# Gated linear attention and a channel mix: the first two 128-token groups joined into one of 256

## The chip, the cores and the metric

One core of one Trainium2 chip. The metric is device time of one execution in microseconds (us), median over runs; lower is better.

## The reference, cut to what matters

```python
# attention: batch 4, heads 8, sequence 768, head size 48
for t in range(S):
    state = alpha[:, :, t, :, None] * state + einsum('bhd,bhe->bhde', k[:, :, t], v[:, :, t])
    y[:, :, t] = einsum('bhd,bhde->bhe', q[:, :, t], state)
# channel mix on x = y as (4, 768, 384), d_ff 1024
x_prev = x shifted by one token
xk = mu_k * x + (1 - mu_k) * x_prev
xr = mu_r * x + (1 - mu_r) * x_prev
k = maximum(xk @ w_k, 0)
out = sigmoid(xr @ w_r) * (k * k @ w_v)
```

## The kernel before

The sequence is cut into chunks of `C` = 128 tokens (24 in all) and the chunks into attention groups (`CUTS`, L29): 13 groups, the first two of one chunk and the others of two. A group's `al`, `k`, `q` and `v` are loaded together (`attention_inputs`, L313). DVE forms running products of alpha by scans along the tokens (`forth` L365, `back` L409), one scan for each of the pairs of heads held, and scales q and k by them (L393). Four pairs of heads go on 128 partitions; three of them fill all rows, and the fourth is stored with its elements spread over the free rows of the three. SP's DMAs gather it into its own place after scaling (`gather`, L431). Group 0 is `DIRECT` (L33): its fourth pair comes straight from DRAM by six more small DMAs (`extra`, L334), and it has four scans each way.

Each chunk then has, on TensorE (PE): transposes of k (`trans` L468, copied out by ACT at L649); an entry, that is the update of the state sums (`update` L485) and the scores (`scores` L497); and a visit, the chunk's outputs (`intra` L513, `inter` L535). DVE masks the scores (L582), advances the state (L613 to L618) and, after a visit, adds the crossed part (`crossed` L570) to what ACT copied out (`leave` L560). For the first four chunks (`JOINED`) entry and visit are separate jobs, and the entry of the next chunk waits for the mask, the copy and the add of this one; later they are one job. Then `spread` (L579) moves the fourth pair's outputs to their partitions by two DMAs.

The channel mix works on groups of its own (`MOES`, L34): group 0 joins the first two attention groups, group 1 is one of 256 tokens, groups 2 to 6 have 512. Of each: a mix (ACT scale L790, DVE blend L793, ACT rounding L796, DVE remainder L799) for xk and for xr; 8 up products of 9 matmuls (`up_ops` L810: high and low halves of fp32 operands) into one of three PSUM tiles `pm`, with relu and squares on ACT (L816 to L822) and a remainder on DVE (L825); 3 gate products of 9 (L835); 3 down products of 24 (L847); and a multiplication by the gate and the store (L970, L975). The down products of group 0 and those after are as wide as the group. In group 0 the mix and the up products are made per attention group, so 128 columns at a time:

```python
            for a in segs:                                    # L1007
                n = GROUPS[a][2] * C
                up_jobs(g, n0, n, w, mix_jobs(g, 0, n0, n, w, [a]))
```

The weights come as raw 64-bit words in ten pieces (4 for w_k, 2 for w_r, 4 for w_v) and are converted in four steps each (`weights`, L729: ACT L744, DVE L752, ACT L760, DVE L764) through two buffers.

The order on every engine is fixed when the kernel is built. `Plan` (L67) holds jobs with an engine, an estimated duration, needs and ring buffers; `order` (L154) simulates them 60 times with varied priorities and keeps the shortest. Engines then run their queues in order. Dummy products on a zero tile keep PE active: `WARM` = 22 at the start (L235), and in every planned gap of PE up to a planned time of `QUIET` = 45 (L1055):

```python
            if plan.start[j] < QUIET and at > 0.0:
                for i in range(int((plan.start[j] - at - 0.2) / 0.2)):
                    PE.matmul(pms[2][:R, :R], zero, zero, start=True, stop=True)
```

Of the kernel before, what the change touches and what calls it, by code (L numbers as in the profile page):

```python
# [25 lines left out]
B, H, S, D = 4, 8, 768, 48  # L26
DM, FF = 384, 1024
C = 128
CUTS = [[1, 1, 2, 2], [2, 2, 2], [2, 2, 2], [2, 2, 2]]  # L29
GROUPS = [(b, sum(cut[:i]), n) for b, cut in enumerate(CUTS) for i, n in enumerate(cut)]  # L30
NA = len(GROUPS)
PLACE = [(0, 0), (0, 1)] + [(i, 0) for i in range(1, NA - 1)]
DIRECT = (0,)  # L33
MOES = [[0, 1], [2], [3, 4], [5, 6], [7, 8], [9, 10], [11, 12]]  # L34
NG = len(MOES)
LMAX = 2 * C
WMAX = 2 * LMAX
NP = H // 2
# [4 lines left out]
NT = 3  # L43
# [5 lines left out]
DW = D // DQ  # L49
NX = HB - D  # L50
NW = 768
WARM = 22
ROUNDS = 60
RAWS = 2
JOINED = 4
QUIET = 45.0


def head(i, o):
# [120 lines left out]
def mm(n):  # L180
    return 0.013 + n / 2400.0 if n > 128 else 0.068
# [6 lines left out]
def act(n, extra=0.0):  # L188
    return 0.13 + n / 1200.0 + extra
# [7 lines left out]
def gated_attention_channel_mix(  # L197
# [17 lines left out]
    PE, ACT, DVE, POOL, SP = nc.tensor, nc.scalar, nc.vector, nc.gpsimd, nc.sync  # L215
# [21 lines left out]
    als, pps, ks, qs = (ring(x, 2, [128, NP * LMAX]) for x in ("al", "pp", "k", "q"))  # L237
    vs = ring("v", 2, [C, 2 * VW])
    for t in (als[0], ks[0], qs[0]):
        POOL.memset(t[:, NT * C : NP * C], 1.0)  # L240
    tiny = cp.tile([128, 1], F32, name="tiny")
    POOL.memset(tiny, FLOOR)
    mone = cp.tile([128, 1], F32, name="mone")
# [32 lines left out]
    tops = [early[:, :NW], *ring("tops", 1, [128, NW], U32)]  # L276
# [19 lines left out]
    plan = Plan()  # L296
    add = plan.add
# [12 lines left out]
    loads, prepped, gathered, half_k, half_q, rescale = {}, {}, {}, {}, {}, {}  # L310
# [150 lines left out]
    def final(a):  # L461
        return a + 1 == NA or GROUPS[a + 1][0] != GROUPS[a][0]

    def trans(i):
        a, c = CH[i]
        k = view(a, ks)
        for p in range(NT):
            PE.transpose(pt[:, p, :], k[:, p, c * C : (c + 1) * C], ident)  # L468
# [141 lines left out]
    def advance(i):  # L610
        a, c = CH[i]
        old, new, nxt = before[i, 0], before[i, 1], marks[i]
        DVE.tensor_tensor(by_pair(new), by_pair(old), grown[:R, 0], op=ALU.add)  # L613
        if nxt is None:
            return
        DVE.tensor_tensor(by_pair(nxt), by_pair(new), grown[:R, 1], op=ALU.add)
        if c == GROUPS[a][2] - 1:
            DVE.tensor_tensor(  # L618
                by_pair(nxt), by_pair(nxt), pes[a % 2][:R].unsqueeze(2).to_broadcast([R, NP, D]),
                op=ALU.mult,  # L620
            )
# [4 lines left out]
    def attention_products():  # L626
        last_mask = last_leave = last_cross = last_adv = last_visit = None
        done = {}
        tcopy = {}

        def slow(i):
            return 1.3 if i < JOINED else 1.0

        def joined_at(i):
            return i >= JOINED

        for i in range(-1, NCH):
            more = i + 1 < NCH
            need = [last_mask, last_adv, last_leave, last_cross, last_visit]
            opened = ()  # L640
            if more:
                a, c = CH[i + 1]
                tr = add(
                    "PE", 0.32 * slow(i), lambda i=i: trans(i + 1), need=[prepped[a]],
                    takes=[("pt", i + 1)], uses=[("k", a)], name=f"trans{i + 1}",
                )

                def keep(i=i):
                    ACT.copy(hts[(i + 1) % 2].rearrange("t (r i) -> t i r", i=NT), pt)  # L649

                tcopy[i + 1] = add(
                    "ACT", act(NT * 128, -0.02), keep, need=[tr], takes=[("ht", i + 1)],
                    uses=[("pt", i + 1)], name=f"ht{i + 1}",
                )
                ready = [tcopy[i + 1], *half_k[a], *half_q[a], *loads[a]["v"]]
                touched = [("ht", i + 1), ("k", a), ("q", a), ("v", a)]
                opened = (0,) if marks[i + 1] is None else (0, 1)
            if i >= 0:
                mine = [("am", i), ("q", CH[i][0]), ("v", CH[i][0]), *before[i]]
            joined = i >= JOINED and more  # L660

            def visit(i=i, out=i >= 0, more=more, opened=opened if joined else ()):
                if more and joined_at(i):
                    update(i + 1, opened)
                if out:
                    intra(i, opened)
                    inter(i, 0)
                    inter(i, 1)
                if more and joined_at(i):
                    scores(i + 1)  # L670

            def enter(i=i, opened=opened):
                update(i + 1, opened)
                scores(i + 1)

            vis = None
            if i >= 0:
                need += ready if joined else []
                vis = add(
                    "PE", (2.28 if joined else 1.5) * slow(i), visit, need=need,  # L680
                    uses=mine + (touched if joined else []), name=f"visit{i}",
                )
                last_visit = vis
                a, c = CH[i]
                last_leave = add(
                    "ACT", 0.5, lambda i=i: leave(i), need=[vis], takes=[("xt", slot_of[a])], name=f"leave{i}"
                )
                last_cross = add(
                    "DVE", 0.42, lambda i=i: crossed(i), need=[vis, last_leave], uses=[("xt", slot_of[a])],
                    name=f"cross{i}",  # L690
                )
                done.setdefault(a, []).append(last_cross)
            if more and not joined:
                a, c = CH[i + 1]
                vis = last_visit = add(
                    "PE", 1.0 * slow(i), enter, need=[*ready, last_mask, last_adv, last_leave, last_cross, last_visit],
                    uses=touched, name=f"enter{i + 1}",
                )
            if more:
                last_mask = add(  # L700
                    "DVE", 0.62, lambda i=i: masked(i + 1), need=[vis], takes=[("am", i + 1)],
                    name=f"mask{i + 1}",
                )
                a, c = CH[i + 1]
                ending = c == GROUPS[a][2] - 1
                last_adv = add(
                    "DVE", 0.62 + (0.25 if ending and not final(a) else 0.0), lambda i=i: advance(i + 1),
                    need=[vis, last_adv, *(rescale.get(a, ()) if ending else ())],
                    takes=[("st", x) for x in held[i + 1]],
                    uses=[before[i + 1][0], *([("pe", a)] if ending else [])], name=f"state{i + 1}",  # L710
                )
            if i >= 0:
                a, c = CH[i]
                if c == GROUPS[a][2] - 1:
                    mv = add(
                        "SP", 0.2, lambda a=a: spread(a), need=done[a], uses=[("xt", slot_of[a])], name=f"spread{a}"
                    )
                    src = [] if GROUPS[a][1] == 0 else [done[a - 1][-1], xready[a - 1][0]]
                    pre = add(
                        "POOL", 0.25, lambda a=a: prefix(a), need=src, takes=[("xt", slot_of[a])],  # L720
                        uses=[("xt", slot_of[a - 1])] if src else [], name=f"prefix{a}",
                    )
                    xready[a] = [mv, *done[a], pre]


    converted = {}
    turn_w = [0]

    def weights(key, f, src, at, hi, lo):  # L729
        n = hi.shape[1] * hi.shape[2]  # L730
# [15 lines left out]
                raw.bitcast(BF16)[:, 4::4], AF.Copy,  # L746
            )

        hb = add("ACT", act(n), head_bits, need=[ld], takes=[("tops", i)], uses=[("raw", i)], name=f"top {key}{f}")

        def join():
            DVE.scalar_tensor_tensor(  # L752
# [139 lines left out]
        return j  # L892

    def up_jobs(g, n0, n, w, xr_):
        slow = 1.6 if g == 0 else 1.0
        for f in range(NF):
            i, pk = acc(n)
            ri = rn[0]
# [5 lines left out]
            def ops(f=f, pk=pk, r=r, k2=k2, dst=dst, xh=xh, xl=xl):  # L904
# [4 lines left out]

            prod, relu = up_ops(f, pk, xh, xl, r, k2, None, None)[:2]  # L910
            jp = pe_job(
                9 * mm(n) * slow, prod, [*xr_, *converted["k", f // 2]], takes=[("pm", i)], uses=[("xk", g)],
                name=f"up{g}.{f}+{n0}",
            )
            jr = add("ACT", act(n, -0.02), relu, need=[jp], takes=[("r", ri)], uses=[("pm", i)], name=f"relu{g}.{f}")
# [131 lines left out]
    for j in late:  # L1047
        plan.need[j] += [k for i in range(turn_w[0]) for x in ("tops", "raw") for k in plan.users[x, i]]

    todo = plan.order(sizes, ROUNDS)  # L1050
    POOL.tensor_scalar(nu, mu, -1.0, 1.0, op0=ALU.mult, op1=ALU.add)
    at = 0.0
    for j in todo:
        if plan.eng[j] == "PE":
            if plan.start[j] < QUIET and at > 0.0:  # L1055
                for i in range(int((plan.start[j] - at - 0.2) / 0.2)):
                    PE.matmul(pms[2][:R, :R], zero, zero, start=True, stop=True)
            at = plan.start[j] + plan.dur[j]
        plan.fn[j]()
    order.close()  # L1060

# [177 lines left out]
```

## Time and profile before

| | us |
|---|---|
| median of 3 runs | 366.55 (364.83 to 367.21) |
| the profiled execution | 367.48 |
| its span, first to last instruction | 365.8 |
| PE busy | 347.4 |
| DVE busy | 225.3 |
| ACT busy | 203.1 |

The profile follows one execution. Times in rows count from the start of the span. A matmul row gives start, duration and the number merged into it; products are pipelined, so their price is the distance between starts and not the duration. fp32 products that are not marked fp32r are recorded twice. PEclk is the clock granted to PE as a share of 2.4 GHz; 0.50 is 1.2 GHz.

### The profile page before, as it was taken

To read this page: it belongs to the slowest core of one execution; us is meant where nothing else is said; L and a number is where in the kernel's file an instruction comes from. 1 tells how busy PE (TensorE), PEld (TensorE's weight loads), DVE (VectorE), ACT (ScalarE), POOL (GpSimd) and SP (SyncE) were. 2 spreads that over 40 slices of the span, in tenths; PEclk is the share of its full clock that TensorE was granted. 3 is DMA by queue.
4 is the path that set the end of the run, shared out by engine and by line. 5 is a ranking of instruction groups with operands and counts; after the bars stand their busy time and mean duration, and the time that the engine had idled before them with its cause. 6 is when DMAs were issued, how large, how long until landed. Compare 5 with 4: busy or idle time off the path is not lost. (4 is left out here: it accounts for less than half of the span.)

```text
span 365.8 us, 10482 instructions
## 1 busy us (share of the span) xinstructions
PE 347.4 (95%) x4469; PEld 301.1 (82%) x4469; DVE 225.3 (62%) x453; ACT 203.1 (56%) x405; POOL 24.6 (7%) x63
## 2 busy tenths in 40 slices
PE   7497999999999999999999999999999999999991
PEld 7387999999999888888888888888888888888780
DVE  5897566587898954659934679517479312743000
ACT  2756565455874993318981349951269731787100
POOL 6110021010000300100000010000000000000000
PEclk9798555599999999999999999999999999999997
DMA  5997705243644202543203443005421001100011
GB/s 182 319 316 227 232 2 185 55 143 82 175 112 125 77 6 62 161 161 90 78 3 104 135 142 110 18 2 126 144 68 39 2 3 42 40 29 0 4 59 35
DMA packets 18295, 35.62 MB, mean 97 GB/s; under 512 B 3776, under 2 KB 9408, under 8 KB 18240
## 3 DMA queue, kind: packets, MB, share of 16 engines
q1 hardware_dynamic: 18096, 34.86, 31.6%
q8 instruction: 37, 0.61, 0.7%
q14 instruction: 18, 0.15, 0.2%
q10 hardware_dynamic: 144, 0.00, 0.0%
HBM read 26.69 MB, written 4.72 MB: 86 GB/s over the span
## 5 line engine op out<-in xcount | busy, mean ns | idle before, releaser
L810 PE MATMUL pm<-xkh,wkh 128*128 128x512 f32 (+2 forms) x192 | 52.5, 388 | 1.6 <-ACT xkh L796 1.6
L810 PE MATMUL pm<-xkl,wkh 128*128 128x512 f32 (+2 forms) x192 | 51.5, 383 | 0.0
L810 PE MATMUL pm<-xkh,wkl 128*128 128x512 f32 (+2 forms) x192 | 51.5, 383 | 0.0
L810 PEld LDWEIGHTS pm<-xkh,wkh 128*128 128x128 f32 x192 | 37.6, 223 | 7.2 <-ACT xkh L796 2.0
L847 PE MATMUL pm<-kb,wvh 128*128 128x512 f32 x120 | 42.2, 404 | 0.0
L810 PEld LDWEIGHTS pm<-xkl,wkh 128*128 128x128 f32 x192 | 38.0, 224 | 4.9
L810 PEld LDWEIGHTS pm<-xkh,wkl 128*128 128x128 f32 x192 | 38.1, 224 | 4.9
L816 ACT ACTIVATE r<-pm 128x512 f32<-128x512 f32 (+2 forms) x64 | 31.1, 486 | 18.4 <-PE pm L810 18.1
L847 PE MATMUL pm<-kha,wvh 128*128 128x512 f32 (+1 forms) x108 | 38.1, 353 | 0.0
L847 PE MATMUL pm<-kla,wvh 128*128 128x512 f32 (+1 forms) x108 | 37.0, 342 | 0.0
L847 PE MATMUL pm<-kha,wvl 128*128 128x512 f32 (+1 forms) x108 | 36.8, 341 | 0.0
L790 ACT ACTIVATE x<-xt,mu 128x512 f32<-128x512 f32 (+2 forms) x48 | 26.3, 609 | 18.4 <-DMA xt<-xt 17.6
L582 DVE TENSOR_TENSOR am<-sp,mask 128x512 f32<-128x512 f32 x24 | 16.5, 688 | 31.6 <-PE sp L497 31.5
L822 ACT ACTIVATE k<-r 128x512 f32<-128x512 f32 (+2 forms) x64 | 32.6, 516 | 1.5 <-DVE kla L825 1.0
L649 ACT COPY ht<-pt 128x384 f32<-128x384 f32 x24 | 16.3, 678 | 30.3 <-PE pt L468 30.2
L793 DVE SCALAR_TENSOR_TENSOR x<-xt,nu,x 128x512 f32<-128x512 f32 (+2 forms) x48 | 27.3, 612 | 5.7 <-ACT x L790 4.9
L825 DVE TENSOR_TENSOR kb<-k,kb 128x512 fp32r<-128x512 f32 x20 | 13.8, 692 | 24.4 <-ACT k L822 14.9
L560 ACT COPY xt<-yu 112x512 f32<-112x512 f32 x24 | 14.0, 584 | 24.6 <-PE yu L535 20.5
L847 PEld LDWEIGHTS pm<-kb,wvh 128*128 128x128 f32 x120 | 22.6, 188 | 5.1
L970 DVE TENSOR_TENSOR sig<-pm,sig 128x512 f32<-128x512 f32 (+1 forms) x21 | 12.8, 611 | 22.3 <-PE pm L847 17.4
L409 DVE TENSOR_TENSOR_SCAN pp<-al,pp 128x255 f32<-128x255 f32 (+1 forms) x40 | 26.3, 690 | 0.3
L365 DVE TENSOR_TENSOR_SCAN pp<-al,tiny 128x256 f32<-128x256 f32 (+1 forms) x40 | 23.6, 630 | 3.3 <-DMA al<-al_p 1.7
(90 smaller groups left out, 630.4 us busy)
## 6 DMA issues: line engine op xcount, KB each, us to landing
v<-v_p SPq DMA_DIRECT2D x11, 400.0 KB, 5.1
al<-al_p SPq DMA_DIRECT2D x11, 384.0 KB, 3.2
q<-q_p SPq DMA_DIRECT2D x11, 384.0 KB, 3.8
k<-k_p SPq DMA_DIRECT2D x11, 384.0 KB, 3.7
out<-sig SPq DMA_DIRECT2D x15, 256.0 KB, 2.1
early<-wk_p SPq DMA_DIRECT2D x4, 768.0 KB, 4.5
early<-wv_p SPq DMA_DIRECT2D x4, 768.0 KB, 4.8
q<-q SPq DMA_DIRECT2D x22, 48.0 KB, 2.3
```

What stands on the lines that cost most here:

```text
L365: DVE.tensor_tensor_scan(view(a, pps)[:, p], view(a, als)[:, p], tiny.to_broadcast([128, n]), initial=START, op0=ALU.mult, op1=ALU.max,)
L409: DVE.tensor_tensor_scan(pp[:, p, 0 : n - 1][:, ::-1], x, x, initial=pp[:, p, n - 1 : n], op0=ALU.mult, op1=ALU.bypass,)
L560: ACT.copy(x[:R].rearrange("r i (s t) -> r i s t", s=2), yu[:R, :, : NP * HC].rearrange("r s (i t) -> r i s t", i=NP),)
L582: DVE.tensor_tensor(ams[i % 2], sp[:, :, : NP * HC].rearrange("c j (p t) -> c j p t", p=NP), mask.unsqueeze(1).unsqueeze(1).to_broadcast([ ...
L649: ACT.copy(hts[(i + 1) % 2].rearrange("t (r i) -> t i r", i=NT), pt)
L790: ACT.activation(x, now, AF.Copy, scale=mu[:, i, t : t + 1])
L793: DVE.scalar_tensor_tensor(x, prev, nu[:, i, t : t + 1], x, op0=ALU.mult, op1=ALU.add)
L810: PE.matmul(pk, w[:, t, cols], x[:, t], start=part == 0 and t == 0, stop=part == 2 and t == NT - 1,)
L816: ACT.activation(r, pk, AF.Relu)
L822: ACT.activation(k2, r, AF.Square)
L825: DVE.tensor_tensor(lo, k2, hi.bitcast(F32), op=ALU.subtract)
L847: PE.matmul(pv, w[f // 2][:, f % 2, cols], x, start=f == 0 and i == 0, stop=f == NF - 1 and i == 2,)
```

## The change

Attention groups 0 and 1, of 128 tokens each, become one of 256, so that all twelve groups have two chunks. No group is `DIRECT`: group 0 holds three pairs like the others, has its fourth gathered, and each group has its own place in the load buffers. The channel mix keeps its seven groups of 256, 256 and five times 512 tokens; the first is now one attention group, mixed and multiplied 256 columns wide. The up products of group 0 are 72 matmuls in place of 144. Dummies: 20 at the start, then as many as fit between a planned time of 8.6 and the first job of PE, and none in later gaps. Some planned durations change, and with them the order.

```diff
-CUTS = [[1, 1, 2, 2], [2, 2, 2], [2, 2, 2], [2, 2, 2]]
+CUTS = [[2, 2, 2]] * 4
-PLACE = [(0, 0), (0, 1)] + [(i, 0) for i in range(1, NA - 1)]
-DIRECT = (0,)
-MOES = [[0, 1], [2], [3, 4], [5, 6], [7, 8], [9, 10], [11, 12]]
+PLACE = [(i, 0) for i in range(NA)]
+DIRECT = ()
+MOES = [[0], [1], [2, 3], [4, 5], [6, 7], [8, 9], [10, 11]]
-WARM = 22
+WARM = 20
+WARMED = 8.6
-QUIET = 45.0
     for t in (als[0], ks[0], qs[0]):
-        POOL.memset(t[:, NT * C : NP * C], 1.0)
+        POOL.memset(t[:, NT * LMAX :], 1.0)
...
-                    "PE", 0.32 * slow(i), lambda i=i: trans(i + 1), need=[prepped[a]],
+                    "PE", 0.26 * slow(i), lambda i=i: trans(i + 1), need=[prepped[a]],
-                    "ACT", act(NT * 128, -0.02), keep, need=[tr], takes=[("ht", i + 1)],
+                    "ACT", 0.61, keep, need=[tr], takes=[("ht", i + 1)],
-                    "DVE", 0.62 + (0.25 if ending and not final(a) else 0.0), lambda i=i: advance(i + 1),
+                    "DVE", 0.75 + (0.3 if ending and not final(a) else 0.0), lambda i=i: advance(i + 1),
-        hb = add("ACT", act(n), head_bits, ...
+        hb = add("ACT", act(n, 0.2), head_bits, ...
-        slow = 1.6 if g == 0 else 1.0
-                9 * mm(n) * slow, prod, [*xr_, *converted["k", f // 2]], ...
+                9 * mm(n), prod, [*xr_, *converted["k", f // 2]], ...
+    filled = set(plan.first["pm", 2])
     todo = plan.order(sizes, ROUNDS)
-    at = 0.0
+    at = WARMED
+    cold = True
     for j in todo:
         if plan.eng[j] == "PE":
-            if plan.start[j] < QUIET and at > 0.0:
-                for i in range(int((plan.start[j] - at - 0.2) / 0.2)):
+            if cold and at == WARMED:
+                for i in range(int((plan.start[j] - at) / 0.19)):
                     PE.matmul(pms[2][:R, :R], zero, zero, start=True, stop=True)
             at = plan.start[j] + plan.dur[j]
+            cold = cold and j not in filled
```

First place, PE from its start to the transposes of the third chunk, before. `zero` marks dummies, `pt` transposes, `yu` and `sp` the tiles of states, outputs and scores:

```order
L235 MATMUL pm_70<-zero 112x112 x22
L468 MATMUL pt<-ident,k_103 128x128 x3
L1057 MATMUL pm_72<-zero 112x112 x2
...
L497 MATMUL sp<-q_105,k_103 64x64 x16
L1057 MATMUL pm_72<-zero 112x112 x9
L513 MATMUL yu<-am_178,v_107 64x64 x16
...
L468 MATMUL pt<-ident,k_103 128x128 x3
L1057 MATMUL pm_72<-zero 112x112 x12
```

The same place of the change:

```order
L235 MATMUL pm_70<-zero 112x112 x20
L1058 MATMUL pm_72<-zero 112x112 x13
L468 MATMUL pt<-ident,k_101 128x128 x6
...
L497 MATMUL sp<-q_103,k_101 64x64 x16
L513 MATMUL yu<-am_176,v_105 64x64 x16
...
L497 MATMUL sp<-q_103,k_101 64x64 x16
L468 MATMUL pt<-ident,k_102 128x128 x3
```

All dummies now stand ahead of the first transposes. The two chunks of group 0 are transposed together, and the scores are followed at once by the visit. The visits of chunks 0, 1 and 2 and the entry of chunk 2 all stand ahead of the first up product; before it was the visits of chunks 0 and 1.

Second place, DVE from the mask of chunk 0 (`am`, L582) to the add behind its visit (`xt`, L570), before:

```order
L582 TENSOR_TENSOR am_178<-sp,mask 128x512
L752 SCALAR_TENSOR_TENSOR early<-early 128x768
L409 SCALAR_TENSOR_TENSOR pp_101<-al_99,pp_101 128x127
L365 SCALAR_TENSOR_TENSOR pp_102<-al_100,tiny 128x256
L393 TENSOR_TENSOR k_103<-k_103,pp_101 128x384
L764 TENSOR_TENSOR wkl_158<-early,wkh_154 128x768
L570 TENSOR_TENSOR xt_180<-xt_180,sp 112x2x64 x2
```

And of the change:

```order
L582 TENSOR_TENSOR am_176<-sp,mask 128x512
L402 RECIPROCAL pp_100<-pp_100 128x3
L752 SCALAR_TENSOR_TENSOR early<-early 128x768
L409 SCALAR_TENSOR_TENSOR pp_100<-al_98,pp_100 128x255 x3
L764 TENSOR_TENSOR wkl_156<-early,wkh_152 128x768
L570 TENSOR_TENSOR xt_178<-xt_178,sp 112x2x64 x2
```

Three scans back of 256 tokens now stand between the two, where there were one of 128, a scan forward and a scaling of k. Both orders have a weight operation and a subtraction of the weights there.

## Rows read from the trace of the kernel before

**Rows 1.** The page's head: the span of the profiled execution.

```profile
span 365.8 us, 10482 instructions
```

**Rows 2.** Busy time by stage, the whole span in five stretches. Columns: from and to (us), length, busy us of PE, PEld (weight loads), DVE, ACT, POOL with the number of instructions, then the granted clock of PE, the DMA share and GB/s.

```profile
0.00:33.57 33.57, 23.13 (x378) 21.62 (x379) 25.15 (x51) 17.84 (x30) 9.16 (x36) 0.90 0.81 261
33.57:74.40 40.83, 40.83 (x355) 40.12 (x356) 26.26 (x66) 24.60 (x79) 3.67 (x3) 0.50 0.43 133
74.40:119.20 44.80, 44.58 (x904) 43.32 (x903) 39.50 (x88) 28.76 (x70) 2.89 (x7) 1.00 0.45 123
119.20:358.20 239.00, 238.86 (x2838) 196.09 (x2836) 133.75 (x252) 131.92 (x230) 8.92 (x17) 1.00 0.22 65
358.20:365.80 7.60, 0.00 (x0) 0.00 (x0) 0.66 (x1) 0.00 (x0) 0.00 (x0) 0.70 0.13 42
```

**Rows 3.** The same view for PE alone around the steps of its clock. Columns: from and to, length, PE busy us and instructions, granted clock, DMA share, GB/s.

```profile
15.00:19.00 4.00, 3.98 (x76) 0.50 0.99 344
20.00:26.00 6.00, 6.00 (x157) 1.00 0.96 296
...
34.00:72.00 38.00, 38.00 (x344) 0.50 0.42 131
...
74.00:75.00 1.00, 1.00 (x9) 0.74 0.11 43
```

**Rows 4.** PE in order of time: start and duration in us, line, tiles, shape, how many; in brackets the idle time ahead and what ended it. Up products (L810) of group 0, then its gate products (L835) at either clock.

```profile
33.57 0.91 PE L810 MATMUL pm<-xkh,wkh 128*128 128x128 f32 x3 [1.64 <-ACT xkh L796]
34.27 0.84 PE L810 MATMUL pm<-xkh,wkl 128*128 128x128 f32 x3
34.91 0.84 PE L810 MATMUL pm<-xkl,wkh 128*128 128x128 f32 x3
...
72.06 0.95 PE L835 MATMUL pm<-xrh,wrh 128*128 128x256 f32 x3
72.81 0.84 PE L835 MATMUL pm<-xrh,wrl 128*128 128x256 f32 x3
73.45 0.84 PE L835 MATMUL pm<-xrl,wrh 128*128 128x256 f32 x3
...
76.97 0.50 PE L835 MATMUL pm<-xrh,wrl 128*128 128x256 f32 x3
77.31 0.50 PE L835 MATMUL pm<-xrl,wrh 128*128 128x256 f32 x3
```

**Rows 5.** The same view, the first row of a visit (L513) or an entry (L485) and the row that follows it, at the low and at the high clock.

```profile
56.52 1.13 PE L513 MATMUL yu<-am,v 64*64 64x64 f32 x32
...
58.44 0.90 PE L810 MATMUL pm<-xkh,wkh 128*128 128x128 f32 x3
...
66.31 0.97 PE L485 MATMUL yu<-v,ht 64*64 64x48 f32 x30
...
68.16 0.90 PE L810 MATMUL pm<-xkh,wkh 128*128 128x128 f32 x3
...
75.44 0.69 PE L513 MATMUL yu<-am,v 64*64 64x64 f32 x32
...
76.52 0.61 PE L835 MATMUL pm<-xrh,wrh 128*128 128x256 f32 x3
...
82.94 0.79 PE L485 MATMUL yu<-v,ht 64*64 64x48 f32 x30
...
84.22 0.38 PE L847 MATMUL pm<-kha,wvh 128*128 128x256 f32 x1
```

**Rows 6.** In order of time: the masks of chunks 0 and 1 on DVE, and the starts of their visits on PE. Dummies stood between them on PE.

```profile
18.39 0.68 DVE L582 TENSOR_TENSOR am<-sp,mask 128x512 f32<-128x512 f32 x1
...
20.88 0.69 PE L513 MATMUL yu<-am,v 64*64 64x64 f32 x32
...
28.18 0.69 DVE L582 TENSOR_TENSOR am<-sp,mask 128x512 f32<-128x512 f32 x1 [0.55 <-PE sp L497]
...
29.81 0.69 PE L513 MATMUL yu<-am,v 64*64 64x64 f32 x32
```

**Rows 7.** In order of time: SP's issue of two of the six small loads of the fourth pair and of the load of k of group 0, and the scaling of that k on DVE.

```profile
1.72 1.33 SPq L334 DMA_DIRECT2D al<-al_p  x2
...
5.94 0.44 SPq L327 DMA_DIRECT2D k<-k_p  x1
...
13.79 0.69 DVE L393 TENSOR_TENSOR k<-k,pp 128x512 f32<-128x512 f32 x1
```

**Rows 8.** Groups of DVE's instructions by line and shape over the span: scans forward (L365) and back (L409), and remainders of the up products (L825). Columns: busy us in all and mean ns of one, then idle time ahead.

```profile
L409 DVE TENSOR_TENSOR_SCAN pp<-al,pp 128x255 f32<-128x255 f32 x33 | 23.3, 737 | 0.2
L365 DVE TENSOR_TENSOR_SCAN pp<-al,tiny 128x256 f32<-128x256 f32 x33 | 21.0, 675 | 1.2 <-DMA al<-al_p 1.2
...
L825 DVE TENSOR_TENSOR kla<-k,kha 128x128 fp32r<-128x128 f32 x16 | 4.3, 284 | 0.3 <-ACT k L822 0.3
...
L825 DVE TENSOR_TENSOR kla<-k,kha 128x256 fp32r<-128x256 f32 x8 | 3.2, 414 | 0.0
...
L365 DVE TENSOR_TENSOR_SCAN pp<-al,tiny 128x128 f32<-128x128 f32 x7 | 2.6, 414 | 2.1 <-POOL st L263 1.5 <-DMA al<-al_p 0.6
```

**Rows 9.** In order of time: SP's issue of the two moves of the fourth pair's outputs (L579) behind chunk 0, and the first reader that waited for them, on POOL (in brackets its idle time ahead).

```profile
23.50 1.28 SPq L579 DMA_DIRECT2D xt<-xt  x2
...
30.34 0.19 POOL L555 COPY xt<-xt 128x3 f32<-128x3 f32 x1 [3.94 <-DMA xt<-xt]
```

More of the change, by code (lines that the diff above doesn't have):

```diff
@@ L747, in head_bits @@
             )
-        hb = add("ACT", act(n), head_bits, need=[ld], takes=[("tops", i)], uses=[("raw", i)], name=f"top {key}{f}")
+        hb = add("ACT", act(n, 0.2), head_bits, need=[ld], takes=[("tops", i)], uses=[("raw", i)], name=f"top {key}{f}")
         def join():
@@ L911, in up_jobs @@
             jp = pe_job(
-                9 * mm(n) * slow, prod, [*xr_, *converted["k", f // 2]], takes=[("pm", i)], uses=[("xk", g)],
+                9 * mm(n), prod, [*xr_, *converted["k", f // 2]], takes=[("pm", i)], uses=[("xk", g)],
                 name=f"up{g}.{f}+{n0}",
```

## Prediction

> **What bounds the kernel now.** I read the stages of the span first [rows 1, 2]. TensorE (PE) is busy in every microsecond from 33.57 us, the first product of the channel mix, to 358.2 us; 7.6 us of close follow. So the end is set by when that dense stretch starts, by the work in it, and by the clock it runs at. The clock column is the second thing to see: from 33.57 to 74.40 us it reads 0.50, the 1.2 GHz level, and DVE is busy for only 26.26 of those 40.83 us. From 119.20 us on, where the products are 512 columns wide, everything runs at 1.00 with DVE at 56%, and the change does not touch that part. Whatever it does is done before 119.20 us.
>
> Then the clock in finer steps [rows 3]. It is 0.50 from 15 to 19 us, 1.00 from 20 us after dummy products, and 0.50 from 34 to 72 us, in which PE's busy share is 38.00 of 38. Being busy alone did not raise it. What runs there are the products of group 0, 128 columns wide. It rises between 74 and 75 us, 2 to 3 us after the first 256-wide products (the gate's, 72.06 us [rows 4]).
>
> Third, the price of one product [rows 4]. Three 128-wide products at the low clock start 0.64 us after the three before them (34.27 to 34.91): 0.213 us each. Three 256-wide ones at the low clock: also 0.64 us (72.81 to 73.45). Three 256-wide ones at 1.00: 0.34 us (76.97 to 77.31), 0.113 us each; I use 0.117, a little above. So a 128-wide product costs as much as a 256-wide one, and a change of width halves the bill.
>
> **The change part by part.** Group 0 now has 256 tokens in one piece. Its up products were 8 x 9 for each half, 144 at 0.213 us = 30.7 us. They become 72 at 0.117 us = 8.4 us: 22.3 us go. Both other products of the group (gate 27, down 72) keep count and width.
>
> In the dense stretch the low clock also slowed other work. An entry of a chunk (state update and scores) takes 66.31 to 68.16 = 1.85 us at the low clock, 82.94 to 84.22 = 1.28 us at the high one; a visit (the outputs) 56.52 to 58.44 = 1.92 us against 75.44 to 76.52 = 1.08 us [rows 5]. The entry of chunk 3 and 9 gate products (9 x 0.096) gain 0.6 + 0.9 = 1.5 us. Entry and visit of chunk 2 and the transposes of chunks 2 and 3 stood in the stretch (2.0 + 2.05 + 0.5 + 0.9 = 5.5 us, with gaps and three dummies); in the new order they stand ahead of the first up product. From the first up product to the last DVE operation it was 358.2 - 33.6 = 324.6 us; it becomes 324.6 - 22.3 - 1.5 - 5.5 = 295.3 us, if the clock is high and PE never waits.
>
> Low clock at the start of the stretch. Without dummies in the gaps I expect 1.2 GHz there. While it lasts, each microsecond does 0.117/0.213 = 0.55 us of work. It lasted 2.5 us with 256-wide products (72.06 to about 74.5, where the mean of 0.74 puts the step) and up to 5 us with dummies (15 to 20 us): 0.45 x 2.5 = 1.1 to 0.45 x 5 = 2.3 us. I take 1.6.
>
> Start of the stretch. Before, 33.57 us, and it needed only the first 128 tokens. Now it needs both chunks. Followed through the new order with durations from the rows: the small loads of the fourth pair are gone, so k is the fourth transfer on SP's queue instead of the tenth (issued at 5.94 us); its scaling on DVE (before 13.79 us) can end near 11 us, after three scans forward, the scaling of q, three scans back and one weight operation [rows 7, 8]. The fourth pair is now gathered by SP after that. This is an added wait: the third weight piece, k of group 1 and its v stand behind it on SP and are issued from some 12.4 us on, about when the third piece went before; and the last scores wait for the gather to land at 14 to 15 us. Entry 0 ends near 16 us, mask 0 near 17.7 us (DVE is full until then; before 19.07). Before, PE sat behind dummies: mask 0 ended at 18.39 + 0.68 = 19.07 and visit 0 began at 20.88 us, mask 1 at 28.87 and visit 1 at 29.81 us [rows 6]: 1.8 and 0.9 us that go. Against that, two entries and two visits run at the low clock, 2 x 0.57 + 2 x 0.84 = 2.8 us. These two nearly cancel. What does not cancel is DVE: between mask 0 and the add behind visit 0 there are now a weight operation, three scans back and a subtraction (0.9 + 3 x 0.7 + 0.9 us), so that add ends near 22 us, entry 1 near 24, visit 1 near 27.6, its add near 29 us. The move of the fourth pair to its partitions took from 23.50 to 30.34 us until its reader went on [rows 9]; with fewer loads ahead of it I take 3.5 to 4 us: it is there at 33 us. Scale, blend and round for three 256-wide tiles, two engines in turn, are some 4 us: first up product at 37 us. Ends: 33.6 (as before) and 41: DVE was busy for 25.15 of the first 33.57 us, 75%; the new order puts some 6 us more of DVE work ahead of this product (three forward scans, mask and state of chunk 2, the last weight halves, a mix twice as wide), and 31/0.75 = 41.
>
> New waits in the stretch. With PE faster, DVE is next. Until 119.20 us it was busy for 25.15 + 26.26 + 39.50 = 90.9 us. The change takes off four scans each way (seven 128-wide forward scans at 0.41 become three at 0.68, back alike), half the remainders (16 x 0.28 to 8 x 0.41) and some mixing: about 5 us [rows 8]. 86 us from 3 us on, at the 88% of the third stage (39.50/44.80), puts the first 512-wide product at 101 us, at 95% at 94 us. PE alone would be there at 37 + 60 = 97 us. I take 3 us of waiting for the pair of them (0 to 6), most likely ahead of the first down product, which needs the last converted weights.
>
> The six removed transfers are small but take SP 1.3 us of issue a pair, 4 us before 8 us [rows 7]; that is in the start above. POOL clears tiles twice as wide, ahead of the first load's landing: nothing, or 0.3 us. The planner's changed costs only reorder.
>
> Sum, in the profiled execution's time: 37 + 295.3 + 1.6 + 3 = 336.9 us to the last DVE operation, + 7.6 of close = 344.5 us span, + 1.7 (367.48 against a span of 365.8) = 346.2 us. That execution was 0.9 us above the median of the runs, so **345 us** against 366.55: 21.5 us or 5.9% less.
>
> The Trainium skill ("TensorE: Matmul & The Clock Gate", "What's actually happening") says that the gate follows how busy PE has been. The 38 us at 0.50 with PE full [rows 3] do not show that for busy time. The same page ("Seeing it yourself") reports the gate stuck at a low level for a long time; by that the low stage would be a stay of the gate that any product can meet, the second rival below.
>
> **Rivals.** (1) DVE sets the pace as poorly as it did: with its share up to 119.20 us, 90.9/119.2 = 76%, its 86 us end at 113 us, and the rest (239.0 us less one visit and entry, 2.3 us, that now come earlier) ends at 349.7: 358 us as a run. For it: waits of DVE for transfers and ACT stay. Against: half of its idle time was waiting for the slow PE. 15%.
> (2) The low clock lasts as long as before, 40.8 us from the first up product: 0.45 x 40.8 = 18.4 us in place of 1.6: 362 us. Against: 256-wide products ended it before within 2.5 us. 3%. **Slower**: the clock stays low until the 512-wide products; 58 us of work take 58/0.55 = 106 us, 48 us more: 391 us. It decides from 51 us of low clock on (0.45 x 51 = 21.5 + 1.6). 2%.
> (3) All is hidden: start at 33.6, no waits, 1 us of clock: 338 us. 15%.
>
> **How the numbers follow.** The forecast with its bounds (start 33.6 to 41, waits 0 to 6) has 65%, rivals 1 and 3 15% each, 2 5%. The range 338 to 355 us reaches from rival 3 to start 41 with waits 6 and a second fall of the clock (41 + 295.3 + 2 x 2.3 + 6, and 8.4 from there to the time of a run); most of rival 1 and all of 2 lie outside. A measurement tells about 1% (3.7 us) from no change; faster by more than that: 0.95, within: 0.03, slower: 0.02.
>
> **What would show it.** Right: up products of group 0 in 72 at some 0.117 us, clock 1.00 from 2 to 5 us after the first of them, that one at 36 to 38 us, the first 512-wide product at 97 to 101 us, DVE over 85% busy between them. Wrong: clock 0.50 beyond 45 us; the first up product after 41 us; PE idle for over 6 us between the two marks; or the stretch from 119.20 us grown from its 239 us less 2.3.

## The result, and the profile after the change

The changed kernel takes **348.08 us** (median of four runs, 346.2 to 348.18) against 366.88 us before (364.83 to 367.96, four runs on the same chip): a ratio of 0.9488 with a 95% interval of 0.944 to 0.9537, so 18.8 us or 5.1% less. 345 had been forecast, with a range of 338 to 355. The profiled execution took 346.2 us, as forecast for it; it was the fastest of its runs, so that the median lies 1.9 us above it and not 0.9 below.

On two chips of the experiments, 5 of 19 executions of the kernel before ended at 358.0 to 360.6 us at a mean clock of 0.947 to 0.954 in place of 0.93, by which they ran some 14 to 19 us less at 1.2 GHz (an estimate from clock and span; no trace of one was kept), so medians of all executions are used for that kernel below, not ratios, except where one is given, and against these shorter ones alone the run called kick gains 7.0 us in place of 12.0.

The page after, answering to [rows 1]: span, busy time by engine, and the granted clock in 40 slices of 8.6 us.

```profile
span 344.5 us, 10124 instructions
...
PE 320.7 (93%) x4345; PEld 273.4 (79%) x4345; DVE 221.1 (64%) x421; ACT 197.3 (57%) x367; POOL 20.4 (6%) x60
...
PEclk9755599999999999999999999999999999999997
```

The stages after, as in [rows 2]: the start to the first up product, the low clock, the rest of the up and gate products of group 0, the stage to the first 512-wide product, and from there to the last DVE operation. Columns: length; busy us of PE, weight loads, DVE, ACT, POOL, each with its instructions; clock; DMA share; GB/s.

```profile
0.00:39.91 39.91, 24.50 (x462) 21.55 (x463) 31.69 (x55) 22.20 (x36) 8.46 (x36) 0.66 0.81 274
39.91:43.56 3.65, 3.65 (x17) 3.65 (x18) 3.65 (x9) 3.65 (x6) 0.00 (x0) 0.50 0.64 217
43.56:56.12 12.56, 12.56 (x215) 12.16 (x215) 12.49 (x25) 12.34 (x32) 0.00 (x0) 1.00 0.75 226
56.12:101.78 45.66, 43.63 (x948) 42.10 (x947) 39.33 (x87) 28.67 (x70) 4.10 (x7) 1.00 0.42 116
101.78:338.34 236.56, 236.36 (x2709) 193.89 (x2707) 133.24 (x250) 130.48 (x227) 7.86 (x17) 1.00 0.22 65
```

In the dense stretch the 40.83 us at 0.50 of [rows 2] have become 3.65 us; ahead of it the mean clock is lower than before, 0.66 in place of 0.90, since no dummies stand in the gaps there (0.87 with them, in a run below). The dense stretch starts 6.3 us later than before, yet the first 512-wide product, the mark behind which nothing was to change, comes at 101.78 in place of 119.20 us: 17.4 us of the gain are there. The stage behind it is 236.56 us, the 239 before less one visit and entry, 2.4 us. Another 1.4 us are in the close after the last DVE operation, 6.2 us in place of 7.6. The span is 21.3 us shorter; the medians differ by 18.8, since the profiled execution before lay above its median and this one below.

The up products of group 0 after, answering to [rows 4]: start, time, engine, line, tiles, count.

```profile
39.91 1.01 PE L810 MATMUL pm<-xkh,wkh 128*128 128x256 f32 x3 [1.53 <-ACT xkh L796]
40.71 0.84 PE L810 MATMUL pm<-xkh,wkl 128*128 128x256 f32 x3
41.35 0.84 PE L810 MATMUL pm<-xkl,wkh 128*128 128x256 f32 x3
...
45.55 0.50 PE L810 MATMUL pm<-xkh,wkl 128*128 128x256 f32 x3
45.89 0.50 PE L810 MATMUL pm<-xkl,wkh 128*128 128x256 f32 x3
```

Start to start, three products take 0.64 us up to the rise of the clock and 0.34 after it: the two prices of the forecast, now for twice the tokens.

### The profile page after: what moved, and what is told of

The parts are those of the page before. It is cut to its first block, busy times and chain, and to the rows that moved or that the text cites. A ratio compares the mean times of both kernels' runs of the same rounds, so it can differ in the third digit from the quotient of the medians.

```text
span 344.5 us, 10124 instructions
## 1 busy us (share of the span) xinstructions
PE 320.7 (93%) x4345; PEld 273.4 (79%) x4345; DVE 221.1 (64%) x421; ACT 197.3 (57%) x367; POOL 20.4 (6%) x60
## 4 chain that ended last, share of the span: by engine, by line
PE 70%; DMA 9%; DVE 9%; ACT 7%; issue 2%; POOL 1%; SPq 1%; ACTq 0%; DVEq 0%
PE pm L847 24%; PE pm L810 24%; PE pm L835 9%; PE yu L485 3%; PE yu L513 3%; DMA xt<-xt 2%; PE sp L497 2%; DMA early<-wk_p 2%; DMA al<-al_p 2%; DMA mu<-mu_p 2%; PE pt L468 2%; ACT x L790 2%; DVE pp L409 2%; PE sp L535 1%; PE yu L535 1%
## 5 line engine op out<-in xcount | busy, mean ns | idle before, releaser
L810 PE MATMUL pm<-xkh,wkh 128*128 128x512 f32 (+1 forms) x168 | 43.8, 370 | 1.5 <-ACT xkh L796 1.5
L810 PE MATMUL pm<-xkh,wkl 128*128 128x512 f32 (+1 forms) x168 | 42.8, 364 | 0.0
L810 PE MATMUL pm<-xkl,wkh 128*128 128x512 f32 (+1 forms) x168 | 42.6, 362 | 0.0
L790 ACT ACTIVATE x<-xt,mu 128x512 f32<-128x512 f32 (+1 forms) x42 | 25.2, 654 | 28.0 <-DMA xt<-xt 28.0
L810 PEld LDWEIGHTS pm<-xkh,wkh 128*128 128x128 f32 x168 | 29.6, 193 | 6.8 <-ACT xkh L796 1.7
L810 PEld LDWEIGHTS pm<-xkh,wkl 128*128 128x128 f32 x168 | 29.9, 193 | 5.0
L816 ACT ACTIVATE r<-pm 128x512 f32<-128x512 f32 (+1 forms) x56 | 29.5, 530 | 7.6 <-PE pm L810 6.9
L810 PEld LDWEIGHTS pm<-xkl,wkh 128*128 128x128 f32 x168 | 29.8, 192 | 4.9
L822 ACT ACTIVATE k<-r 128x512 f32<-128x512 f32 (+1 forms) x56 | 31.5, 565 | 3.2 <-DVE kla L825 2.3
L825 DVE TENSOR_TENSOR kb<-k,kb 128x512 fp32r<-128x512 f32 x20 | 13.9, 693 | 24.2 <-ACT kb L819 12.9
L582 DVE TENSOR_TENSOR am<-sp,mask 128x512 f32<-128x512 f32 x24 | 16.4, 683 | 17.8 <-PE sp L497 17.8
L793 DVE SCALAR_TENSOR_TENSOR x<-xt,nu,x 128x512 f32<-128x512 f32 (+1 forms) x42 | 26.4, 665 | 1.5 <-ACT x L790 1.3
L847 PEld LDWEIGHTS pm<-kb,wvh 128*128 128x128 f32 x120 | 22.6, 188 | 5.0
L365 DVE TENSOR_TENSOR_SCAN pp<-al,tiny 128x256 f32<-128x256 f32 x36 | 22.8, 675 | 4.8 <-DMA al<-al_p 4.8
L409 DVE TENSOR_TENSOR_SCAN pp<-al,pp 128x255 f32<-128x255 f32 x36 | 25.2, 736 | 0.5 <-DVE pp L402 0.2
```

Source lines behind the costliest of these rows:

```text
L365: DVE.tensor_tensor_scan(view(a, pps)[:, p], view(a, als)[:, p], tiny.to_broadcast([128, n]), initial=START, op0=ALU.mult, op1=ALU.max,)
L409: DVE.tensor_tensor_scan(pp[:, p, 0 : n - 1][:, ::-1], x, x, initial=pp[:, p, n - 1 : n], op0=ALU.mult, op1=ALU.bypass,)
L582: DVE.tensor_tensor(ams[i % 2], sp[:, :, : NP * HC].rearrange("c j (p t) -> c j p t", p=NP), mask.unsqueeze(1).unsqueeze(1).to_broadcast([ ...
L790: ACT.activation(x, now, AF.Copy, scale=mu[:, i, t : t + 1])
L793: DVE.scalar_tensor_tensor(x, prev, nu[:, i, t : t + 1], x, op0=ALU.mult, op1=ALU.add)
L810: PE.matmul(pk, w[:, t, cols], x[:, t], start=part == 0 and t == 0, stop=part == 2 and t == NT - 1,)
```

## Experiments

Every kernel is an edit of the one before or of the changed one. The summary (medians; T is the start of the first up product, M that of the first 512-wide one, in each profiled execution). They were run on several chips; medians of the kernel before differ between chips by up to 2.3 us (364.55 to 366.88), and T differs by 0.2 us between the changed kernel's two traces:

| kernel | what differs | us | T | M |
|---|---|---|---|---|
| changed | | 348.1 | 39.91 | 101.78 |
| changed, again | other chip | 348.1 | 40.11 | 103.11 |
| halves in group 0 | changed, 128 wide there | 369.5 | 40.06 | 125.08 |
| halves in group 1 | changed, 128 wide there | 353.1 | 40.10 | 108.25 |
| kick | before, 20 dummies inside group 0 | 352.5 | 33.28 | 107.18 |
| dummies alone | before, the new rule | 367.0 | 33.77 | 118.69 |
| dummies in gaps | changed, the old rule | 348.5 | 40.88 | 103.74 |
| wide alone | before, up products 256 wide | 359.0 | 37.58 | 109.33 |
| all but the joining | before, wide, dummies, costs | 353.4 | 44.11 | 107.26 |
| old costs | changed, old planner costs | 352.0 | 40.70 | 103.80 |
| factors later | changed | 346.4 | 39.39 | 101.42 |
| join later | changed | 347.2 | 39.22 | 102.61 |
| spread first | changed | 348.8 | 40.00 | 106.30 |

**Width: halves in group 0.** The theory was that 128-wide products cost double per token and leave the clock low; the rival, that the joined groups and the start had made the gain.

```
-                    PE.matmul(pk, w[:, t, cols], x[:, t], ...)
+                    for z in halves:      # columns 0:128, 128:256, in group 0 only
+                        PE.matmul(pk[:, z], w[:, t, cols], x[:, t, z], ...)
```

> The changed kernel, but each up product of group 0 is made as two of 128 columns: 144 instead of 72, in the same jobs, with every other engine's instructions in the same order. My theory (a 128-wide product costs what a 256-wide one costs at the 1.2 GHz level, and as long as they run the clock stays there): the clock reads 0.50 from the first up product (39.9 us) until 2 to 4 us into the gate products, each product takes 0.213 us, 30.7 us in place of 8.4, and entry, visit and gate products beside them run at the low clock too (1.5 to 2.5 us): 348 + 24 = 372 us, between 367 and 376. Rival (the gain came from the joined attention groups and the start, the clock rises whatever runs): the clock rises within 5 us, and 144 products at 0.06 to 0.117 us cost 8.6 to 16.8 us: 348 to 357 us.

369.46 us (368.68 to 373.25): 21.4 us back, as my theory had it and not the rival; 22.3 were forecast for count and clock together, and some 1.5 for what runs beside these products. (Both halves are summed side by side in one bank, which changes the sums of that group; what is timed is the products.) Busy PE and clock:

```profile
50.00:60.00 10.00, 10.00 (x48) 0.50 0.41 120
60.00:70.00 10.00, 10.00 (x75) 0.50 0.14 39
70.00:78.00 8.00, 8.00 (x76) 0.50 0.44 115
78.00:80.00 2.00, 2.00 (x19) 0.98 0.00 0
```

The reader sees PE full and the clock at 1.2 GHz for 38 us, from T on, as in [rows 3], in a kernel that differs from the changed one in product width alone. The Trainium skill ("TensorE: Matmul & The Clock Gate", "What's actually happening") lets the clock follow how busy PE has been; here equal busy shares stand beside either level, so PE's busy time as the profile records it does not tell the level in these rows.

**Halves in group 1**, the same edit with `g == 1`, entered at the high clock.

> The changed kernel, but the up products of group 1 (not 0) are made in halves of 128 columns, entered with the clock at 1.00. My theory (these products do not hold the clock): it falls back to 0.50 within the 144 products, which then take 0.213 us each: 10 to 22 us more, 358 to 371 us. Rival (the clock has only to be raised once and stays): it reads 1.00 throughout, the products take 0.06 to 0.117 us: 0 to 8.4 us more, 348 to 357 us; the price of a 128-wide product at 2.4 GHz is then read from their starts.

353.14 us (352.4 to 353.8), 5.0 more: the rival was right, and my theory's second half fell. The clock did not fall back:

```profile
72.00:76.00 4.00, 4.00 (x38) 1.00 0.21 80
76.00:80.00 4.00, 4.00 (x144) 1.00 0.19 26
80.00:84.00 4.00, 4.00 (x38) 1.00 0.56 204
84.00:88.00 4.00, 4.00 (x38) 1.00 0.13 25
```

The 128-wide products in that stretch, six to a row:

```profile
72.48 0.83 PE L811 MATMUL pm<-xkh,wkh 128*128 128x128 f32 x6
73.15 0.83 PE L811 MATMUL pm<-xkh,wkl 128*128 128x128 f32 x6
73.82 0.83 PE L811 MATMUL pm<-xkl,wkh 128*128 128x128 f32 x6
```

0.67 us for six is 0.112 each, beside 0.113 to 0.117 for a 256-wide one. So at either level a 128-wide product costs what a 256-wide one costs, and in these two kernels such products neither raised nor lowered the clock. Of the 8.1 us that 72 products more cost at 0.112, 5.0 show in the time: PE waits less, 0.4 us from T to M in place of 2.0.

By these prices the change of group 0 is 144 x 0.213 - 72 x 0.112 = 22.6 us. How it splits depends on the order: with the clock first, 144 x (0.213 - 0.112) = 14.5 us are the clock's and 8.1 the count's; with the count first, 72 x 0.213 = 15.3 are the count's and 7.3 the clock's. Why a 128-wide product costs as much as one of twice the width stays open. The profile records a weight load beside each product ([rows 2]: 356 beside 355), and no run here tells the load from the product.

**Clock alone: the kick.** If that is so, a push inside the stretch (dummy products that raise the clock) must give most of the clock's 14.5 us with no change of width.

```
+        if plan.name[j] == "up0.2+0":          # kernel before
+            for i in range(20):
+                PE.matmul(pms[2][:R, :R], zero, zero, start=True, stop=True)
         plan.fn[j]()
```

> The kernel before, with 128-wide up products throughout; the only edit is 20 dummy products (112 columns) put ahead of the third up product group of group 0, inside the dense stretch. My theory after the two halves runs (128-wide products keep the clock at whichever level it is, and cost 0.213 or 0.112 us by it): the dummies take 2.5 to 4 us, the clock rises behind them some 7 us after the first up product and stays, 126 products save 0.101 us each (12.7 us) and the entries, visits and gate products beside them 2 to 3 us: 367 + 3.5 - 15 = 355 us, between 351 and 361, with no change of width at all. Rival (128-wide products pull the clock down again): 366 to 371 us.

352.52 us (351.2 to 355.19), against a median of 364.55 for the kernel before on that chip: 12.0 less. From T to M its trace has 73.90 us, where that of the kernel before has 85.63: 11.7 less. The products around the dummies:

```profile
36.06 0.84 PE L810 MATMUL pm<-xkl,wkh 128*128 128x128 f32 x3
36.70 6.01 PE L1061 MATMUL pm<-zero 112*112 112x112 f32 x40
42.48 0.53 PE L810 MATMUL pm<-xkh,wkh 128*128 128x128 f32 x3
42.85 0.50 PE L810 MATMUL pm<-xkh,wkl 128*128 128x128 f32 x3
43.18 0.49 PE L810 MATMUL pm<-xkl,wkh 128*128 128x128 f32 x3
```

And the clock:

```profile
33.28:40.00 6.72, 6.72 (x36) 0.54 0.67 192
40.00:42.00 2.00, 2.00 (x19) 0.84 0.88 273
42.00:44.00 2.00, 2.00 (x22) 1.00 1.03 418
44.00:61.50 17.50, 17.50 (x315) 1.00 0.37 115
```

The dummies cost 5.8 us, more than the 2.5 to 4 I gave them; the clock rises within them, the same 128-wide products then go at 0.33 in place of 0.64 us per three, and it stays up. One edit of three lines gives nearly two thirds of the change's gain.

So 128-wide products stay at the low clock once they have it; what brought it is another question. In the kernel before it was high up to the first of them (columns as in [rows 3]):

```profile
32.00:33.00 1.00, 0.00 (x0) 1.00 0.76 252
33.00:34.00 1.00, 0.43 (x2) 0.78 0.76 172
```

It fell within half a microsecond of T, behind a stop of PE of 1.64 us ([rows 4]); in the kick, too, it was high up to T and fell there. With dummies up to T in the changed kernel (the old rule, below) it did not fall. But the changed kernel also has a stop of 1.68 us ahead of 89.69 us, at 1.00, and no fall behind it. So what brings the fall is not shown, and the kernel before with its stop filled was not run.

**The dummies' rule.** In the kernel before the new rule alone (20, then up to the first transposes); in the changed one the old rule added (`plan.start[j] < 45.0`, up to the first product into the third `pm` tile).

> The kernel before with the change's rule for dummies alone: 20 and then as many as the plan leaves up to the first transposes, none in later gaps. My theory: group 0 stays at 0.50 for some 40 us as before; visits no longer stand behind dummies (1.8 and 0.9 us), entries and visits run at the low clock (2.8 us): 363 to 370 us, middle 367. Rival (the dummies in the gaps cost the time): under 362 us.

366.99 us; the ratio to the kernel before is 1.0026 (1.0002 to 1.0049): same, as costed. Here the clock was at 0.50 ahead of T already, and the low stage ended as before, near 74 us.

> The changed kernel with dummy products in the gaps of the early visits again, by the rule of the kernel before (68 of them after the first transposes). My theory: the clock is high in the entries and visits and at the first up product (1.6 us of low clock go, 2.8 us in visits and entries of which about half is on the path), but visits stand behind dummies for 1 to 2 us: 345 to 350 us, middle 347. Rival (the dummies are what held the kernel before): 351 us or more.

348.46 us (348.41 to 349.28), no change. Its dense stretch, and that of the changed kernel as run again:

```profile
40.88:103.74 62.86, 59.36 (x1176) 56.66 (x1177) 54.30 (x116) 43.63 (x104) 3.71 (x7) 1.00 0.50 141
```

```profile
40.11:103.11 63.00, 60.67 (x1177) 58.46 (x1178) 55.73 (x118) 44.73 (x106) 3.94 (x7) 0.96 0.48 142
```

With the clock high from the first product PE is busy 1.3 us less, and the stretch is as long: PE waits 3.5 us in place of 2.3. So what is left of the low clock is hidden behind waits for inputs, and DVE, busy for 54.30 of the 62.86 us, is not far behind PE.

**Width alone** in the kernel before: both mixes, then `up_jobs(g, 0, w, w, mixed)`.

> The kernel before with one edit alone: the up products of group 0 are made once, 256 wide, after both 128-token mixes; attention groups of one chunk, the fourth-pair loads and the dummies in gaps stay. My theory (width and clock carry the gain): 72 products at 0.117 us, clock high from 2 to 5 us after the first (or at once, behind dummies), first up product 37 to 41 us: 344 to 355 us, middle 349. Rival (joining the attention groups carries it): over 358 us.

358.97 us (358.19 to 361.49), in the rival's range (over 358) and 10 us above the middle of mine: 7.2 us below the kernel before on that chip (366.15). PE between T and M, its busy time and clock (columns as in the stages above):

```profile
37.58:109.33 71.75, 64.57 (x1182) 62.36 (x1183) 61.83 (x131) 48.68 (x114) 3.96 (x9) 0.91 0.48 141
```

And its costliest wait (us in all, times, longest):

```profile
PE yu L485 <- ACT ht L649: 7.1, 4, 4.2
```

PE waited 7.1 us for the transposed k of later chunks, and the clock was low for some 13 of the 71.75 us: 6.3 us from T on, and again from 54 to 61 us, behind the longest of these waits. T is 2.3 us earlier than in the changed kernel and M 7.6 later. So width alone does not carry the gain: it needs inputs that come in time.

**All but the joining**: that edit, the new dummies and the new planner costs.

> The kernel before with wide up products of group 0, and also the change's dummies and planner costs: all of the change but the joining of the first two attention groups and the fourth-pair loads. My theory after the run with wide products alone (359 us; PE waited 7 us for the inputs of later attention groups and the clock was low for some 6 us): the joined groups give the rest, 355 to 361 us. Rival (dummies and costs gave the rest): 347 to 351 us.

353.44 us (352.43 to 354.94): just under the range of my theory and above the rival's. Ahead of its first up product PE stood still:

```profile
40.48 0.90 PE L469 MATMUL pt<-ident,k 128*128 128x128 f32 x3 [9.47 <-DVE k L394]
43.56 0.90 PE L469 MATMUL pt<-ident,k 128*128 128x128 f32 x3 [2.18 <-ACT ht L650]
44.11 0.99 PE L811 MATMUL pm<-xkh,wkh 128*128 128x256 f32 x3
```

The transposes of chunk 2 wait in PE's queue, and the products behind them, for DVE to scale k of a third group; joined, chunk 2 is the second group's. From T to M it takes 63.15 us, like the changed kernel's 63.00, and M to the last DVE operation 236.9 against 236.5. So the joining, with the fourth pair's loads that go with it, is worth 4.0 us at T and 1.6 in the close (from the start of the last DVE operation to the end of the span: 351.7 - 344.1 = 7.6, against 345.6 - 339.6 = 6.0): 5.6, where the medians say 5.3.

**The planner's costs** of the kernel before in the changed one (0.32 for the transposes, 0.62 for the states, `act(n)` for the tops, 1.6 on the up products).

> The changed kernel with the planner's costs of the kernel before (transposes, hidden-state copy, states, tops, factor 1.6 on the up products of group 0), which gives another order on every engine. My working put these costs at nothing: 346 to 350 us. Rival (the costs carry part of the gain): 351 us or more.

351.95 us (350.78 to 352.06), so 3.8 us hang on them. The rival was right. Its two stages, T to M and from M on:

```profile
40.70:103.80 63.10, 58.53 (x1048) 56.26 (x1049) 55.71 (x119) 44.26 (x105) 4.22 (x7) 0.97 0.47 140
103.80:343.41 239.61, 238.95 (x2838) 196.00 (x2836) 133.35 (x250) 131.13 (x229) 7.58 (x17) 1.00 0.22 65
```

As many microseconds to M, but with 129 matmuls fewer: one visit and entry stay behind M, and the last stage is 3.1 us longer. The costs "only reorder", and the order is worth 1%.

**The start of the stretch: three trials.** First, POOL's mixing factors issued behind `ends1`, so that DVE's reciprocal needn't wait for POOL, which waits for their load.

> The changed kernel; POOL's product of the mixing factors (which waits 1.62 us for their load) is issued behind the ends of group 1 instead of ahead of the ends of group 0, so that DVE's reciprocal of group 0 need not wait for it. My theory (this wait of 1.37 us is what put the scaling of k 1.5 us behind the time I forecast, and the start of the stretch hangs on the chain behind it in part): the scaling of k ends at 11.1 instead of 12.5 us, and the first up product comes 0.3 to 1.4 us earlier: 346.7 to 347.8 us. Rival (the chain is held by the landing of the fourth weight piece and of the spread): no change of the start, 348 us.

346.42 us (346.01 to 347.01), the best kernel of the study. In the changed kernel:

```profile
7.68 0.20 POOL L1051 TENSOR_SCALAR nu<-mu 128x6 f32<-128x6 f32 x1 [1.62 <-DMA mu<-mu_p]
...
8.40 0.18 DVE L402 RECIPROCAL pp<-pp 128x3 f32<-128x3 f32 x1 [1.37 <-POOL pe L383]
...
32.42 1.29 SPq L579 DMA_DIRECT2D xt<-xt  x2
...
36.73 0.51 ACT L790 ACTIVATE x<-xt,mu 128x256 f32<-128x256 f32 x1 [2.70 <-DMA xt<-xt]
```

And with the factors later:

```profile
7.64 0.18 DVE L402 RECIPROCAL pp<-pp 128x3 f32<-128x3 f32 x1 [0.40 <-POOL pe L383]
...
31.10 1.29 SPq L579 DMA_DIRECT2D xt<-xt  x2
...
36.20 0.51 ACT L790 ACTIVATE x<-xt,mu 128x256 f32<-128x256 f32 x1 [3.12 <-DMA xt<-xt]
```

The spread [rows 9] goes out 1.3 us earlier and is used 0.5 earlier. (The median is 1.7 us below the changed kernel's, more than T moved, but from another chip: how much of that is the edit's isn't settled.) So the transfer holds a part back; does it wait for those queued ahead of it? The next run moves it ahead of them.

> The changed kernel; on SP the spread of group 0 to its partitions is issued ahead of the loads of q and v of group 2 instead of behind them, nothing else is moved. My theory (the start of the dense stretch at 39.9 us hangs on the landing of the spread, 4.3 us after its issue, because 784 KB stand ahead of it): the spread lands 1 to 2 us earlier, the first up product is at 38 to 39 us, 346 to 347.5 us against 348.1. Rival (the start hangs on mask 2 and visit 2, or on the mix itself): the first up product within 0.4 us of 39.9 and 348 us, or slower by the later q and v.

348.82 us (347.61 to 350.88), T 40.00: no gain in time. But the transfer did get shorter:

```profile
33.19 1.91 SPq L579 DMA_DIRECT2D xt<-xt  x2
...
36.82 0.51 ACT L790 ACTIVATE x<-xt,mu 128x256 f32<-128x256 f32 x1 [2.62 <-DMA xt<-xt]
```

From issue to use it took 3.6 us, where it takes 4.3 and 4.9 us in the two traces of the changed kernel. So the loads ahead of it cost some 0.7 to 1.3 us; T did not follow, because in this execution the spread went out 0.8 us later (33.19 for 32.42), as k of group 0 was already scaled 0.5 us later. PE's waits from T to M grew to 4.0 us, at transposed k and at the mix; whether the later q and v of group 2 did that is not shown. What makes up the 3.6 us that are left, for two moves of 48 KB, stays open.

> The changed kernel with POOL's mixing factors behind the ends of group 1 (as in the run before) and, on DVE and ACT, the joining and rounding of the fourth weight piece put behind mask 1, so that the scaling of k of group 1 no longer stands behind the wait for that piece (1.2 to 1.3 us on DVE). My theory (the start of the dense stretch is set by the chain mask 0, scaling of k of group 1, mask 1, visit 1, spread; each microsecond of it is one at the end): the spread is issued 2 to 3 us earlier than in the changed kernel, the first up product at 37 to 38.5 us, 344 to 346.5 us. Rival (the landing of the spread is held by the transfers queued ahead of it, or the later work of DVE and ACT sets the pace): the first up product moves by less than 0.8 us, 346 to 348 us.

347.21 us (345.62 to 347.35) against 348.13 (347.33 to 349.58) for the changed kernel on the same chip; T 39.22, so most of the expected gain did not come. The third trial also puts the fourth weight piece's joining behind mask 1 and has the rival's result. DVE between mask 1 and the add behind visit 1:

```profile
25.47 0.68 DVE L582 TENSOR_TENSOR am<-sp,mask 128x512 f32<-128x512 f32 x1
26.07 0.95 DVE L752 SCALAR_TENSOR_TENSOR early<-early,tops 128x768 uint32<-128x768 uint32 x1
28.00 0.96 DVE L764 TENSOR_TENSOR wkl<-early,wkh 128x768 fp32r<-128x768 f32 x1 [0.97 <-ACT wkh L760]
28.87 1.27 DVE L365 TENSOR_TENSOR_SCAN pp<-al,tiny 128x256 f32<-128x256 f32 x2
30.06 0.93 DVE L752 SCALAR_TENSOR_TENSOR early<-early 128x768 uint32<-128x768 uint32 x1
30.91 0.48 DVE L570 TENSOR_TENSOR xt<-xt,sp 112x128 f32<-112x128 f32 x2
```

Mask 1 is 2.4 us earlier than in the changed kernel (27.91), the add 1.0 (31.87): one weight operation more (L752 at 26.07) now stands between them on DVE, and the wait for ACT (0.97 us at 28.00) only moved behind the mask.

## Why the prediction was right, and where not

- **The bound, right.** It read group 0 at the low clock as the place, and everything from M on as untouched: 236.56 us where 239 less 2.3 was said.
- **Count and clock, right in sum.** 22.3 us forecast and 1.5 beside them, 21.4 taken back by halves alone; prices 0.213 and 0.113 to 0.117 us as used. That the clock by itself is worth much, the forecast could not say and the kick showed: 12.0 us with no change of width. Nor is the width worth as much everywhere: in the kernel before, width alone gave 7.2 us, with 7.1 us of waits for transposed k and a second fall of the clock in the stretch.
- **Low clock at the start, right.** 3.65 us within the 2.5 to 5 said, at 0.45 each 1.6 us. In other traces with wide products in group 0 it lasted 2.8 to 6.3 us from T on, and with dummies in the gaps of the changed kernel 0, so the 1.6 holds for this execution and not for each.
- **Start of the stretch, wrong by 2.9 us** (39.91 for 37, inside the bounds 33.6 to 41, outside the 36 to 38 named as a sign). I followed the chain from operation to operation. It met a wait of POOL for a load (1.37 us on DVE) and one for the fourth weight piece (1.29), neither of them in my working: k was scaled at 12.5 us ([rows 7]: 13.79 before; 11 said), the add behind visit 1 ended at 32.3 (29). But taking these waits away moved T by 0.5 and 0.9 us only. The upper bound had the better reason: DVE has 31.69 us of work ahead of T (31 said), 79% of the time. That this load is what slowed the chain is argued, not shown.
- **New waits, too high by 1 us.** 2.0 us from T to M (61.87 less 59.84 busy, 3 said), at transposes and transposed k, not at the down products. From T to the last DVE operation it was 298.4 us, where 295.3 + 1.6 + 3 = 299.9 stood.
- **Close, taken over as 7.6, was 6.2.** It is 7.3 to 7.6 in every trace with one-chunk groups and fourth-pair loads, 6.0 to 6.2 in every one without; why stays open.
- So the sum of 344.5 us for the span was met exactly because +2.9, -1.5 and -1.4 cancel, which is luck, and not because each term was right. The median, 348.08, is 3.1 us above the 345 forecast, as this execution was the fastest.
- **"The planner's changed costs only reorder", wrong:** 3.8 us. The sum was not harmed, as it was made on the new order, with the visit that comes ahead of M.
- **Dummies at no net cost, right** both ways. **Rival 1** (DVE as poor as before) fell: DVE was busy for 55.5 of the 61.87 us from T to M, 90%. The argument against it was weaker than it read: up to 119.20 us in the kernel before, waits for PE make only 6.8 of DVE's 28.3 idle us, and waits for ACT about twice as much. **The second rival's** long stay at the low clock did not come with wide products in any trace here.

## What to carry to other kernels

Read the price of one product and the granted clock of its stretch apart: a stage can be full and still run at half the clock, and then both the width and a short push inside the stage are levers. Measure a start by the next mark that all work must pass: a T 6.5 us earlier (37.58 against 44.11) brought M 2.1 us later. Ahead of T, where DVE had 79% of the stretch as work, taking a wait of 1.37 us away brought T forward by 0.5 us, and taking that and one of 1.29 us away by 0.9 us: a wait on the chain is not worth its length.

## What the hardware showed that I had not expected

- A 128-wide product of these operands costs as much as a 256-wide one at both levels: 0.213 and 0.213 us, 0.112 and 0.113 to 0.117 us.
- In the changed kernel such products left the clock where they found it: 0.50 for 38 us with PE full, 1.00 for the whole of group 1. In the kernel before and the kick it fell as they began, behind a stop of PE, and stayed down for 41 us in the one; in the other 20 dummies of 112 columns (each recorded twice), 5.8 us of them, raised it, and it stayed up. Where the clock was low with 256-wide products it was up again 2.8 to 6.3 us after T.
- A move of 2 x 48 KB took 4.3 to 5.1 us from issue to use behind 784 KB of loads on its queue, and 3.6 us ahead of them.
